# First stage of a transformer block: modulation weights in segments of 256, 384 and 384 features in place of four of 256, with the scale half of each segment used ahead of its shift half

## The chip, the cores and the metric

The kernel runs on one core of a Trainium2 chip. The metric is the time of one execution in device microseconds (us). Executions of an unchanged kernel lie mostly within about 1 us of one another, so medians are quoted with their ranges.

In the profile, PE is TensorE (PEld its weight loads), DVE is VectorE, ACT is ScalarE, POOL is GpSimd, and SPq is the queue that issues the loads. PSUM is the memory that matmuls write to, in banks.

**K** is the start of the first K matmul, **V** the start of the first V matmul.

## The reference

```python
mod = (silu(c) @ w_mod).reshape(..., 6, ...)      # sa, ca, ga, sb, cb, gb: 1024 values each
h = layernorm(x) * (1 + ca) + sa                  # x is 2048 x 1024
x = x + ga * linear_attention(h, wqkv, wo)        # q, k, v = h @ wqkv, 32 heads
h = layernorm(x) * (1 + cb) + sb
x = x + gb * (gelu(h @ w_gate) * (h @ w_up) @ w_down)
```

The first K matmul needs h, h needs the scale ca and the shift sa, and these are two blocks of columns of `silu(c) @ w_mod`. Their weights are 4 MB. So at the start nothing useful can run on TensorE until part of w_mod has been loaded and multiplied.

## The kernel before

The 1024 features are 8 blocks of 128 (called features 0 to 7 here), and a chunk is 128 rows of x. The modulation weights come in four segments of 256 features, each with a shift half (`t=0`) and a scale half (`t=1`). For each segment TensorE runs 32 small matmuls ("passes"; weights 128x128, one moving column), DVE copies the four result columns out of PSUM and adds 0 or 1, DVE modulates the transposed, normalised chunks of x for the two features, and then the K matmuls of these features can run. All K matmuls of chunks 0 to 3 stay open in seven PSUM banks and 496 of the 512 columns of bank 4 until feature 7 is done; the other 16 columns of bank 4 take the results of the passes.

```python
        def wmq_dma(q, ts=(0, 1)):
            for t in ts:
                sch.dma(Q, lambda e, t=t: e.dma_start(WMQ[q][:, :, t, :], wm_v[:, :, t * D + q * 256:t * D + (q + 1) * 256]), ...)
# ... (cut)
        x_dma(0, 1)
        x_dma(1, 2)
        wmq_dma(0, (1,))
        x_dma(2, 3)
        wmq_dma(0, (0,))
        x_dma(3, 4)
        w_dma(WK, OFF_WK, "wk", 1, 0, D, 0, 2)        # Wk, features 0 and 1
        for q in range(1, 4):
            wmq_dma(q)
            # ... Wk of features 2q, 2q+1
# ... (cut)
        def mod_cols(q, bank):       # the 32 passes of a segment
            for t in range(2):
                for b in range(2):
                    for dc in range(NDC):
                        # PS(bank, col) += WMQ[q][:, dc, t, b*128:...] x SILUT[:, dc]
        def mod_copy(q, bank):       # PSUM columns + (0 or 1) -> MODT, on DVE
# ... (cut)
        k_part(0, [2])               # K matmuls of segment 0, chunk 2
        xhat_dve(3, *xh_buf(3))      # normalise chunk 3 (DVE)
        mod_cols(1, 4)
        mod_copy(1, 4)
        t1(3, 7)                     # transpose chunk 3 (PE), copy it out of PSUM (ACT)
        mod1(0, 3, 2, 4)             # modulate chunks 0-2, features 2-3 (DVE)
        k_part(1, [0, 1, 2])
        mod1(3, 1, 0, 4)             # modulate chunk 3, features 0-3
        k_part(0, [3])
        k_part(1, [3])
        mod_cols(2, 4)
        mod_copy(2, 4)
        warm(2)                      # two matmuls on zeros that keep PE busy
        mod1(0, 4, 4, 6)
        k_part(2, [0, 1, 2, 3])
        mod_cols(3, 4)
        mod_copy(3, 4)
        mod1(0, 4, 6, 8)
        # K matmuls of features 6 and 7, then the evacuations and V
```

## Time and profile before

| | before |
|---|---|
| median of 3 runs | 839.61 us (838.99 to 839.78) |
| span of the profiled run | 836.8 us |
| first K matmul (K) | 11.34 |
| first V matmul (V) | 31.57 |
| K to V | 20.23 us |
| V to the end | 805.21 us |

From the page of the kernel before: the span, the busy line, and the first line of the chain of waits (shares of the span by engine).

```profile
span 836.8 us, 11359 instructions
...
PE 830.2 (99%) x4194; PEld 384.4 (46%) x4194; DVE 511.7 (61%) x895; ACT 336.1 (40%) x555; POOL 37.1 (4%) x91
...
PE 98%; DMA 1%; DVE 1%; SPq 0%; ACT 0%; issue 0%
...
```

And the busy times by stretch, from V to the end (columns: stretch, its length, then busy us and instruction count of PE, weight loads, DVE, ACT and POOL, granted clock, DMA share, GB/s):

```profile
...
31.57:837.00 805.43, 802.72 (x3942) 370.19 (x3938) 494.50 (x843) 327.51 (x544) 31.81 (x67) 1.00 0.48 129
...
```

TensorE is busy 802.7 of 805.4 us after V. The longest extra distance between two matmul starts there is 0.1 us. What is left to gain lies ahead of V.

The timeline of PE in the first stage (start, length with the modelled end of the last matmul, what, count, and in brackets idle time and what ended it). L602 are passes, L680 and L756 K (or V) matmuls, L736 warm-up matmuls on zeros, L546 transposes:

```profile
...
9.20 0.95 PE L602 MATMUL ps_all<-siluT,wmq 128*128 128x1 bf16 x32 [0.59 <-DMA wmq<-in_w_mod_dram]
...
11.34 1.02 PE L680 MATMUL ps_all<-wk,h1T 128*128 128x512 bf16 x4
...
14.27 1.04 PE L680 MATMUL ps_all<-wk,h1T 128*128 128x512 bf16 x4 [0.17 <-DVE h1T L565]
15.14 0.94 PE L602 MATMUL ps_all<-siluT,wmq 128*128 128x1 bf16 x32
...
16.76 2.98 PE L680 MATMUL ps_all<-wk,h1T 128*128 128x512 bf16 x13 [0.20 <-DVE h1T L565]
...
21.06 0.94 PE L602 MATMUL ps_all<-siluT,wmq 128*128 128x1 bf16 x32
...
22.71 1.69 PE L680 MATMUL ps_all<-wk,h1T 128*128 128x512 bf16 x7 [0.25 <-DVE h1T L565]
...
26.16 0.94 PE L602 MATMUL ps_all<-siluT,wmq 128*128 128x1 bf16 x32
27.81 3.30 PE L680 MATMUL ps_all<-wk,h1T 128*128 128x512 bf16 x14 [0.71 <-DVE h1T L565]
...
31.57 2.75 PE L680 MATMUL ps_all<-wv,h1T 128*128 128x512 bf16 x12
...
```

Four things are to be seen. The passes of segment 0 wait for their shift load. The first K part starts at 11.34; the trace has Wk's first piece landing at 11.20. Chunk 2's part (14.27) and each of the three later segments (16.76, 22.71, 27.81) begin with idle time that DVE ends. None of these four idle times is a wait for data from memory.

The chain of waits for the last segment (start, length, what):

```profile
...
26.32 0.79 PE ps_all L602 x32
...
27.14 0.17 DVE modt L611
...
27.34 0.42 DVE h1T L565
...
27.81 3.30 PE ps_all L680 x14
...
```

Last pass, 0.17 us copy, 0.42 us for modulating the first feature of four chunks, then K: that round trip is what a segment costs beyond its passes. Bracketed idle times leave out the modelled end of the matmul before, so I count idle time below as the distance between two matmul starts less the usual one (0.216 us after a full matmul, 0.055 after a transpose, 0.025 after a pass). The Trainium skill, "TensorE: Matmul & The Clock Gate", section "Wait — 56ns, not 53.3ns?", has the first (215.7 ns at 512 columns) and the last (a floor of about 25 ns). For before this gives 0.33 us at chunk 2, 0.37 at segment 1, 0.41 at segment 2 (after two warm-up matmuls), 0.85 at segment 3 and 0.11 more at feature 7: 2.07 us.

### The profile page before, as it was taken

How to read it: one execution, taken by the hardware profiler on the slowest of the kernel's cores; microseconds unless marked ns; L12 is line 12 of the kernel's file. 1: busy time of each engine (PE TensorE's matmuls, PEld its weight loads, DVE VectorE, ACT ScalarE, POOL GpSimd, SP SyncE). 2: the span in 40 equal slices, each digit the busy share in tenths (PEclk: the TensorE clock that was granted, in tenths of full speed). 3: DMA queues.
4: the chain of work that ended last, by engine and by line, in shares of the span. 5: the costliest groups of instructions: out<-in, count | busy, mean ns of one | idle time of the engine just before them, and what ended most of it. 6: DMA issues, size and time to landing. Idle time of an engine off the chain costs nothing.

```text
span 836.8 us, 11359 instructions
## 1 busy us (share of the span) xinstructions
PE 830.2 (99%) x4194; PEld 384.4 (46%) x4194; DVE 511.7 (61%) x895; ACT 336.1 (40%) x555; POOL 37.1 (4%) x91
## 2 busy tenths in 40 slices
PE   8999999999999999999999999999999999999998
PEld 4444444444444444444444444444444444444445
DVE  6678877687785577753455665356556535655512
ACT  2357777446423355420354442045554104445300
POOL 2012111000200000010000000000000000000000
DMA  9984422239696769180555533055553305555000
GB/s 291 312 251 101 102 76 76 78 79 235 140 236 204 224 202 277 28 194 26 158 151 151 152 101 76 19 158 152 151 151 101 76 20 159 152 154 145 7 19 26
DMA packets 184102, 113.22 MB, mean 135 GB/s; under 512 B 35560, under 2 KB 175080, under 8 KB 183024
## 3 DMA queue, kind: packets, MB, share of 16 engines
q1 hardware_dynamic: 184032, 112.50, 50.0%
q8 instruction: 33, 0.54, 0.3%
q14 instruction: 21, 0.17, 0.1%
q10 hardware_dynamic: 16, 0.00, 0.0%
HBM read 100.67 MB, written 4.47 MB: 126 GB/s over the span
## 4 chain that ended last, share of the span: by engine, by line
PE 98%; DMA 1%; DVE 1%; SPq 0%; ACT 0%; issue 0%
PE ps_all L1144 23%; PE ps_all L1116 23%; PE ps_all L1119 23%; PE ps_all L680 13%; PE ps_all L1059 7%; PE ps_all L721 7%; PE ps_all L702 1%; DMA wmq<-in_w_mod_dram 1%; PE ps_all L961 0%; PE ps_all L602 0%; DVE h1T L565 0%; PE ps_all L973 0%; PE ps_all L756 0%; PE ps_all L643 0%; SPq L442 0%; DVE st L742 0%
## 5 line engine op out<-in xcount | busy, mean ns | idle before, releaser
L1116 PE MATMUL ps_all<-h2T,wg 128*128 128x512 bf16 x896 | 339.6, 379 | 0.0
L1119 PE MATMUL ps_all<-h2T,wu 128*128 128x512 bf16 x896 | 339.6, 379 | 0.0
L1144 PE MATMUL ps_all<-wd,yT 128*128 128x512 bf16 (+3 forms) x952 | 194.2, 366 | 0.0
L1127 ACT ACTIVATE q<-ps_all 128x512 f32<-128x512 f32 x112 | 66.9, 597 | 225.3 <-PE ps_all L1116 221.5
L1144 PEld LDWEIGHTS ps_all<-wd,yT 128*128 128x128 bf16 x952 | 90.1, 98 | 103.9 <-issue 0.4
L1116 PEld LDWEIGHTS ps_all<-h2T,wg 128*128 128x128 bf16 x896 | 87.7, 98 | 105.8 <-issue 0.2
L1119 PEld LDWEIGHTS ps_all<-h2T,wu 128*128 128x128 bf16 x896 | 87.7, 98 | 105.7
L1132 DVE SCALAR_TENSOR_TENSOR ww<-th,guh 128x512 f32<-128x512 f32 x112 | 77.5, 692 | 77.9 <-ACT th L1131 77.9
L1129 DVE SCALAR_TENSOR_TENSOR ww<-q,ps_all 128x512 f32<-128x512 f32 x112 | 76.9, 686 | 77.7 <-ACT guh L1128 77.6
L1131 ACT ACTIVATE th<-ww 128x512 f32<-128x512 f32 x112 | 70.5, 629 | 87.3 <-DVE ww L1129 87.3
L1149 DVE TENSOR_TENSOR ps_all<-ps_all,gbb 128x512 f32<-128x512 f32 (+3 forms) x34 | 22.7, 667 | 94.8 <-PE ps_all L1144 94.8
L1134 DVE TENSOR_TENSOR yT<-ww,ps_all 128x512 bf16<-128x512 f32 x112 | 76.8, 686 | 3.8
L1128 ACT ACTIVATE guh<-ps_all 128x512 f32<-128x512 f32 x112 | 66.3, 592 | 0.0
L721 PE MATMUL ps_all<-h1T,wq 128*128 128x512 bf16 x256 | 58.7, 379 | 0.0
L680 PE MATMUL ps_all<-wk,h1T 128*128 128x512 bf16 x248 | 57.3, 379 | 1.3 <-DVE h1T L565 1.3
L669 ACT ACTIVATE eb<-ps_all 128x512 f32<-128x512 f32 x64 | 37.4, 600 | 50.6 <-PE ps_all L680 22.3
L680 PE MATMUL ps_all<-wv,h1T 128*128 128x512 bf16 x256 | 57.7, 379 | 0.0
L1059 PE MATMUL ps_all<-w,pq 128*128 128x512 bf16 x256 | 56.2, 379 | 0.0
L670 DVE TENSOR_SCALAR eb<-eb 128x512 f32<-128x512 f32 x64 | 27.1, 423 | 26.7 <-ACT eb L669 26.3
L1059 PEld LDWEIGHTS ps_all<-w,pq 128*128 128x128 bf16 x256 | 25.0, 98 | 30.2 <-issue 0.2
L680 PEld LDWEIGHTS ps_all<-wv,h1T 128*128 128x128 bf16 x256 | 24.9, 98 | 29.5
L680 PEld LDWEIGHTS ps_all<-wk,h1T 128*128 128x128 bf16 x248 | 23.8, 98 | 30.6 <-DVE h1T L565 3.1
(96 smaller groups left out, 481.0 us busy)
## 6 DMA issues: line engine op xcount, KB each, us to landing
wg<-in_B_w_gate_dram SPq DMA_DIRECT2D x56, 512.0 KB, 4.1
wu<-in_B_w_up_dram SPq DMA_DIRECT2D x56, 512.0 KB, 5.3
rb<-scr_rd SPq DMA_DIRECT2D x32, 256.0 KB, 6.6
wd<-in_B_w_down_dram SPq DMA_DIRECT2D x7, 1024.0 KB, 8.5
wmst<-in_w_mod_dram SPq DMA_DIRECT2D x6, 1024.0 KB, 6.8
wmq<-in_w_mod_dram SPq DMA_DIRECT2D x8, 512.0 KB, 7.7
out_dram<-xall SPq DMA_DIRECT2D x31, 128.0 KB, 1.7
xall<-in_A_x_dram SPq DMA_DIRECT2D x3, 1024.0 KB, 12.4
```

The source lines that it names most:

```text
L680: o = sch.op(T, lambda e, dc=dc: e.matmul(PS(bank), H1[sg][:, dc, ci * P:(ci + 1) * P], W_[:, dc, jg * 512:(jg + 1) * 512], start=(dc == 0 ...
L721: o = sch.op(T, lambda e, dc=dc: e.matmul(PS(b), WQ[:, dc, qc * P:(qc + 1) * P], H1[sg][:, dc, :], start=(dc == 0), stop=(dc == NDC - 1)), ...
L1059: last[half] = sch.op(T, lambda e, g=g, half=half: e.matmul(PS(b0 + half), PQ[sg][:, g, ci * P:(ci + 1) * P], W2[:, g, half * 512:(half + ...
L1116: og = sch.op(T, lambda e, dc=dc: e.matmul(PS(bg), WG[slot][:, dc, e_ * P:(e_ + 1) * P], H2[sg][:, dc, :], start=(dc == 0), stop=(dc == ND ...
L1119: ou = sch.op(T, lambda e, dc=dc: e.matmul(PS(bu), WU[slot][:, dc, e_ * P:(e_ + 1) * P], H2[sg][:, dc, :], start=(dc == 0), stop=(dc == ND ...
L1127: sch.op(A, lambda e: e.activation(Q1[j][:, :], PS(bg), ACTF.Square, scale=math.sqrt(GELU_A)), prd=pr(bg), wr=rq, note=f"q1 {fc}")
L1128: ogh = sch.op(A, lambda e: e.activation(GUH[j][:, :], PS(bg), ACTF.Copy, scale=0.5), prd=pr(bg), wr=rg, note=f"gh {fc}")
L1129: sch.op(V, lambda e: e.scalar_tensor_tensor(WW[j][:, :], Q1[j][:, :], 1.0, PS(bg), op0=ALU.add, op1=ALU.mult), rd=rq, prd=pr(bg), wr=rw, ...
L1131: sch.op(A, lambda e: e.activation(TH[j][:, :], WW[j][:, :], ACTF.Tanh, scale=GELU_C), rd=rw, wr=rt, note=f"th {fc}")
L1132: sch.op(V, lambda e: e.scalar_tensor_tensor(WW[j][:, :], TH[j][:, :], 1.0, GUH[j][:, :], op0=ALU.add, op1=ALU.mult), rd=rt + rg, wr=rw, n ...
L1134: sch.op(V, lambda e: e.tensor_tensor(YT[:, fc, :], WW[j][:, :], PS(bu), ALU.mult), rd=rw, prd=pr(bu), wr=r_yt(fc), note=f"yT {fc}")
L1144: o = sch.op(T, lambda e, b=b, fc=fc, c0=c0, c1=c1, n=n: e.matmul(PS(b, 0, n), YT[:, fc, ci * P:(ci + 1) * P], WDT[fc // 4][:, fc % 4, c0:c1],
```

## The change

Three segments of 2, 3 and 3 features need one round of copy and modulation less. Each scale half is multiplied ahead of its shift half, without waiting for it. Loads of 384 features have 768 B packets in place of 512 B. To have K work between the two halves, chunk 3's transpose moves ahead of segment 1, and its K parts of features 0 and 1 stand between the halves. Two smaller parts: after each later copy DVE modulates chunk 0 alone first, and one K matmul of chunk 3 is kept back as filler behind the last copy.

```diff
-        WMQ = [at(f"wmq{i}", [P, NDC, 2, 256], bf16, MSO[i]) for i in range(4)]
+        SEG = [(0, 2), (2, 5), (5, 8)]
+        SGO = [OFF_MS3, OFF_WS, OFF_WS + 12288]
+        WMQ = [at(f"wmq{i}", [P, NDC, 2, (d1 - d0) * P], bf16, SGO[i]) for i, (d0, d1) in enumerate(SEG)]
 # ... (loads: scale, then shift, of each segment, then its Wk features; cut)
         warm(6, 7)
-        mod_cols(0, 4)
+        mod_cols(0, 1, 4)
+        mod_cols(0, 0, 4)
 # ... (cut)
         xhat_dve(3, *xh_buf(3))
-        mod_cols(1, 4)
-        mod_copy(1, 4)
         t1(3, 7)
-        mod1(0, 3, 2, 4)
-        k_part(1, [0, 1, 2])
-        mod1(3, 1, 0, 4)
+        mod1(3, 1, 0, 2)
+        mod_cols(1, 1, 4)
         k_part(0, [3])
         k_part(1, [3])
-        mod_cols(2, 4)
-        mod_copy(2, 4)
+        mod_cols(1, 0, 4)
+        mod_copy(1, 4)
+        mod1(0, 1, 2, 3)
+        mod1(1, 3, 2, 3)
+        mod1(0, 4, 3, 5)
         warm(2)
-        mod1(0, 4, 4, 6)
-        k_part(2, [0, 1, 2, 3])
-        mod_cols(3, 4)
-        mod_copy(3, 4)
+        k_part(2, [0, 1, 2, 3])
+        k_part(3, [0, 1, 2, 3])
+        mod_cols(2, 1, 4)
+        k_part(4, [0, 1, 2])
+        mod_cols(2, 0, 4)
+        mod_copy(2, 4)
+        mod1(0, 1, 5, 6)
+        mod1(1, 3, 5, 6)
         mod1(0, 4, 6, 8)
+        kv_mm(3, "k", 0, kb0[3, 0], [4])
+        k_part(5, [0, 1, 2])
+        kv_mm(3, "k", 0, kb0[3, 0], [5])
 # ... (features 6 and 7, and chunk 3's second half of features 4 to 7; cut)
```

In the new kernel `k_part` takes one feature, not a segment of two.

More of the change, by code (lines that the diff above doesn't have):

```diff
@@ L297, in bass_adaLN_cond__linear_attn_block__geglu_ffn__prompt_kernel @@
             ("c8", [NDC, P], bf16, 256), ("cT", [P, NDC], f32, 64), ("chalf", [P, NDC], f32, 64),
-            ("thc", [P, NDC], f32, 64), ("siluT", [P, NDC], bf16, 64), ("modt", [P, 16], f32, 64), ("add4", [P, 4], f32, 64),
+            ("thc", [P, NDC], f32, 64), ("siluT", [P, NDC], bf16, 64), ("modt", [P, 16], f32, 64), ("add6", [P, 6], f32, 64),
             ("sbT", [P, NDC], f32, 64), ("cb1T", [P, NDC], f32, 64),
@@ L312, in bass_adaLN_cond__linear_attn_block__geglu_ffn__prompt_kernel @@
         SBT, CB1T, CBT, ZCOLS = (_small[k] for k in ("sbT", "cb1T", "cbT", "zcols"))
-        MODT, ADD4 = _small["modt"], _small["add4"]
+        MODT, ADD6 = _small["modt"], _small["add6"]
         NEGHALF, STA, MVA, RSA, NMA, VEA = (_small[k] for k in ("neghalf", "st", "mv", "rs", "nm", "ve"))
@@ L357, in r_wmq @@
         def r_wmq(i, t):
-            return [(MSO[i] + (dc * 2 + t) * 512, MSO[i] + (dc * 2 + t + 1) * 512, f"wmq{i}") for dc in range(NDC)]
+            w = (SEG[i][1] - SEG[i][0]) * P * 2
+            return [(SGO[i] + (dc * 2 + t) * w, SGO[i] + (dc * 2 + t + 1) * w, f"wmq{i}") for dc in range(NDC)]
         R_WARM = [(OFF_GUH, OFF_GUH + 1024, "warm")]
@@ L449, in w_dma, with wmq_dma @@
                            wr=[t_ for dc in range(dc0, dc1) for t_ in r_w(off, name, dc, c0, c1)], note=f"{name}.{dc0}.{c0}")
-        def wmq_dma(q, ts=(0, 1)):
-            for t in ts:
-                sch.dma(Q, lambda e, t=t: e.dma_start(WMQ[q][:, :, t, :], wm_v[:, :, t * D + q * 256:t * D + (q + 1) * 256]),
-                        wr=r_wmq(q, t), note=f"wmq{q}.{t}")
+        def wmq_dma(q, t):
+            d0, d1 = SEG[q]
+            sch.dma(Q, lambda e: e.dma_start(WMQ[q][:, :, t, :], wm_v[:, :, t * D + d0 * P:t * D + d1 * P]), wr=r_wmq(q, t), note=f"wmq{q}.{t}")
         sch.op(V, lambda e: e.memset(WARM[:], 0.0), wr=R_WARM, note="warm")
-        sch.op(V, lambda e: e.memset(ADD4[:, 0:2], 0.0), wr=r_sm("add4"), note="add4")
-        sch.op(V, lambda e: e.memset(ADD4[:, 2:4], 1.0), wr=r_sm("add4"), note="add4")
+        sch.op(V, lambda e: e.memset(ADD6[:, 0:3], 0.0), wr=r_sm("add6"), note="add6")
+        sch.op(V, lambda e: e.memset(ADD6[:, 3:6], 1.0), wr=r_sm("add6"), note="add6")
         x_dma(0, 1)
         x_dma(1, 2)
-        wmq_dma(0, (1,))
+        wmq_dma(0, 1)
         x_dma(2, 3)
-        wmq_dma(0, (0,))
+        wmq_dma(0, 0)
         x_dma(3, 4)
         w_dma(WK, OFF_WK, "wk", 1, 0, D, 0, 2)
-        for q in range(1, 4):
-            wmq_dma(q)
-            for d0, d1 in ((2, 4),) if q == 1 else ((2 * q, 2 * q + 1), (2 * q + 1, 2 * q + 2)):
+        for q, ds in ((1, ((2, 4), (4, 5))), (2, ((5, 6), (6, 7), (7, 8)))):
+            wmq_dma(q, 1)
+            wmq_dma(q, 0)
+            for d0, d1 in ds:
                 w_dma(WK, OFF_WK, "wk", 1, 0, D, d0, d1)
@@ L575, in mods_act, with r_modt @@
                        rd=r_h1(sg, dc, dc + 1, s0, s1) + rs_, wr=r_h1(sg, dc, dc + 1, s0, s1), note=f"h1moda {sg}.{s0}.{dc}")
+        SEGD = [(q, d0, d1) for q, (d0, d1) in enumerate(SEG) for _ in range(d0, d1)]
+        def r_modt(q):
+            d0, d1 = SEG[q]
+            return [(SMO["modt"] + 8 * d0, SMO["modt"] + 8 * d1, "modt")]
         def sc1(dc):
-            k = (dc // 2) * 4 + dc % 2
-            return MODT[:, k + 2:k + 3], MODT[:, k:k + 1], r_smc("modt", dc // 2, 16)
+            q, d0, d1 = SEGD[dc]
+            k = d0 + dc
+            return MODT[:, k + d1 - d0:k + d1 - d0 + 1], MODT[:, k:k + 1], r_modt(q)
         def sc2(dc):
@@ L593, in bass_adaLN_cond__linear_attn_block__geglu_ffn__prompt_kernel, with mod_cols @@
         MC0 = 496
-        def mod_cols(q, bank):
+        def mod_cols(q, t, bank):
             o = None
-            rng = [(bank * 2048 + (MC0 + q * 4) * 4, bank * 2048 + (MC0 + q * 4 + 4) * 4)]
-            for t in range(2):
-                for b in range(2):
-                    col = MC0 + q * 4 + t * 2 + b
-                    for dc in range(NDC):
-                        o = sch.op(T, lambda e, t=t, b=b, dc=dc, col=col: e.matmul(
-                            PS(bank, col, col + 1), WMQ[q][:, dc, t, b * P:(b + 1) * P], SILUT[:, dc:dc + 1],
-                            start=(q == t == b == dc == 0), stop=(dc == NDC - 1), skip_group_check=True),
-                            rd=r_wmq(q, t) + r_sm("siluT"), pwr=(rng if dc == 0 else ()), note=f"mod{q}.{t}.{b}.{dc}")
+            d0, d1 = SEG[q]
+            c0 = MC0 + 2 * d0 + t * (d1 - d0)
+            rng = [(bank * 2048 + c0 * 4, bank * 2048 + (c0 + d1 - d0) * 4)]
+            for b in range(d1 - d0):
+                for dc in range(NDC):
+                    o = sch.op(T, lambda e, b=b, dc=dc: e.matmul(
+                        PS(bank, c0 + b, c0 + b + 1), WMQ[q][:, dc, t, b * P:(b + 1) * P], SILUT[:, dc:dc + 1],
+                        start=(q == b == dc == 0 and t == 1), stop=(dc == NDC - 1), skip_group_check=True),
+                        rd=r_wmq(q, t) + r_sm("siluT"), pwr=(rng if dc == 0 else ()), note=f"mod{q}.{t}.{b}.{dc}")
             for t_ in rng:
@@ L609, in mod_copy @@
         def mod_copy(q, bank):
-            rng = [(bank * 2048 + (MC0 + q * 4) * 4, bank * 2048 + (MC0 + q * 4 + 4) * 4)]
-            sch.op(V, lambda e: e.tensor_tensor(MODT[:, q * 4:q * 4 + 4], PS(bank, MC0 + q * 4, MC0 + q * 4 + 4), ADD4[:, :], ALU.add),
-                   prd=rng, rd=r_sm("add4"), wr=r_smc("modt", q, 16), note=f"modcp{q}")
+            d0, d1 = SEG[q]
+            n = d1 - d0
+            rng = [(bank * 2048 + (MC0 + 2 * d0) * 4, bank * 2048 + (MC0 + 2 * d1) * 4)]
+            sch.op(V, lambda e: e.tensor_tensor(MODT[:, 2 * d0:2 * d1], PS(bank, MC0 + 2 * d0, MC0 + 2 * d1), ADD6[:, 3 - n:3 + n], ALU.add),
+                   prd=rng, rd=r_sm("add6"), wr=r_modt(q), note=f"modcp{q}")
         MT = (4, 5, 6, 7, 8, 9)
@@ L761, in k31, with k_part @@
                 sch.ps.set_writer(*rng[0], o)
-        def k_part(q, cs):
-            for dc in (2 * q, 2 * q + 1):
-                for (c_, jg), b in kb0.items():
-                    if c_ in cs:
-                        kv_mm(c_, "k", jg, b, [dc])
-                if 3 in cs:
-                    k31([dc])
+        def k_part(dc, cs):
+            for (c_, jg), b in kb0.items():
+                if c_ in cs:
+                    kv_mm(c_, "k", jg, b, [dc])
+            if 3 in cs:
+                k31([dc])
         warm(11, 7)
@@ L791, in bass_adaLN_cond__linear_attn_block__geglu_ffn__prompt_kernel @@
         k_part(0, [0])
+        k_part(1, [0])
         xhat_dve(2, *xh_buf(2))
@@ L798, in bass_adaLN_cond__linear_attn_block__geglu_ffn__prompt_kernel @@
         k_part(0, [1])
+        k_part(1, [1])
         mod1(2, 1, 0, 2)
@@ L801, in bass_adaLN_cond__linear_attn_block__geglu_ffn__prompt_kernel @@
         k_part(0, [2])
+        k_part(1, [2])
         xhat_dve(3, *xh_buf(3))
-        mod_cols(1, 4)
-        mod_copy(1, 4)
         t1(3, 7)
-        mod1(0, 3, 2, 4)
-        k_part(1, [0, 1, 2])
-        mod1(3, 1, 0, 4)
+        mod1(3, 1, 0, 2)
+        mod_cols(1, 1, 4)
         k_part(0, [3])
         k_part(1, [3])
-        mod_cols(2, 4)
-        mod_copy(2, 4)
-        warm(2)
-        mod1(0, 4, 4, 6)
-        k_part(2, [0, 1, 2, 3])
-        mod_cols(3, 4)
-        mod_copy(3, 4)
+        mod_cols(1, 0, 4)
[3 more added lines that the diff above has]
+        mod1(0, 4, 3, 5)
+        warm(2)
+        k_part(2, [0, 1, 2, 3])
[3 more added lines that the diff above has]
+        mod_cols(2, 0, 4)
+        mod_copy(2, 4)
+        mod1(0, 1, 5, 6)
+        mod1(1, 3, 5, 6)
         mod1(0, 4, 6, 8)
+        kv_mm(3, "k", 0, kb0[3, 0], [4])
+        k_part(5, [0, 1, 2])
+        kv_mm(3, "k", 0, kb0[3, 0], [5])
         for (c_, jg), b in kb0.items():
             kv_mm(c_, "k", jg, b, [6, 7])
-        k31([6, 7])
+        k31([4, 5, 6, 7])
         k31(list(range(NDC)), MC0, 512)
```

## The prediction

> **What bounds the kernel now.** TensorE: the page has PE busy 99% of the span, the chain of waits 98% PE. Listing PE instructions by start, from the first V matmul (31.57 us) to the end there is no idle over 0.1 us. So only the first stage can move the time: total = start of V + 805 us. The change touches nothing after it.
>
> The first stage, before (timeline): warm-up; wait for the first w_mod segment (landed 9.15, passes at 9.20); first K matmul at 11.33, when the first Wk piece had just landed (11.20); then only latency chains. PE idles 0.34 us before chunk 2's K part, 0.2 in each of segments 1 and 2 (warm-up matmuls hide more of the latter), 0.7 before segment 3. These chains are: last pass, copy to modt, modulation on DVE, K matmul, about 0.8 us each. Nothing on PE after 11.33 waits for a DMA.
>
> **What the change does.** Pass count stays 128 (25 ns apart, the floor that the Trainium skill states in "TensorE: Matmul & The Clock Gate", section "Wait — 56ns, not 53.3ns?"; the trace agrees), K matmuls 64 at 216 ns, warm-ups 25. Removed: one copy/modulate round of four. The scale half of each segment runs before the shift half lands. DMA: 4 MB still, but 768 B packets in four loads. From 27 ns at 512 B and 46 at 1 KB in the trace I estimate 37 ns at 768 B: 2.4 us per load, about 1 us less DMA time in all.
>
> **On the critical path.** Estimates from trace durations, in the new PE order:
> - Segment 0 finishes 0.4 us earlier, but four warm-ups follow and the first K matmul still needs Wk, landing 11.20: K starts at 11.3, gain at most 0.1. Chunk 2's part still starts near 14.2-14.3 (ACT copy 1.02 us, then DVE).
> - T1 of chunk 3 follows directly (15.1), then 24 scale passes (0.6), then chunk 3's K parts of features 0-1. These need the transpose drained, the ACT copy (1.02) and DVE (0.3): ready at 17.1-17.2, PE free at 16.1. A new bubble of about 1.0 us.
> - 24 shift passes, to 18.65; copy, modulate chunk 0 alone (128 wide, 0.31); K at 19.4, idle 0.3 after two warm-ups.
> - 16 K matmuls, 24 passes, 6 K, 24 passes, to 25.35; one K matmul as filler, idle 0.5; K of feature 5 at 26.1; 7+14+4 matmuls and the 16-column rest: V at 31.6-31.7.
>
> The saved round (about 0.7 us) pays for the new bubble and little remains: net -0.2 to +0.3 us. Estimated landings leave over 1 us of slack at every later load (shift of segment 1 lands at 16.0, needed 18; of segment 2 at 22.9, needed 24.8), also with the 1.5 us by which one DMA engine lagged before, after a 16 KB instruction fetch.
>
> **Prediction: 839.6 us**, 838.6 to 840.6 in 8 of 10. Faster by over 2%: 0.003; within 2%: 0.994; slower by over 2%: 0.003.
>
> **What would show it.** V's first matmul at 31.4-31.9; first K at 11.3; a PE gap of 1 us before chunk 3's first K matmul, released by DVE modulation; gaps of 0.3 and 0.5 after the two later copies; 768 B packets near 37 ns; no PE wait on a DMA after 11.33; the rest unchanged.
>
> **What would make it wrong.** 768 B packets costing as much as 1 KB (46 ns): the last shift load would land at 25-27 and stall PE up to 2 us. The warm-up ending at another moment. A lowered PE clock after the longer stretch of small passes and idle at 15-17 us. A gain of 0.5-1 us if chunk 3's transpose, copy and modulation overlap better than I count.

## More of the kernel before

`k31`, which `k_part` calls for chunk 3 (not shown), is the second half of chunk 3's K. It shares PSUM bank 4 with the pass results, so it may not run while DVE copies those out.

## The result, and the profile after

| | before | after |
|---|---|---|
| median of 6 runs | 839.3 us (838.66 to 839.78) | 839.02 us (838.69 to 839.51) |
| ratio | | 0.9997, 95% interval 0.9984 to 1.001 |
| span of the profiled run | 836.8 | 837.7 |
| first Wk piece lands | 11.20 | 11.99 |
| K | 11.34 | 12.12 |
| V | 31.57 | 32.49 |
| K to V | 20.23 | 20.37 |
| V to the end | 805.21 | 805.21 |

A ratio is the mean time of one kernel's runs over that of the other's of the same rounds, so not quite the ratio of the medians.

The profiled execution of after is even 0.9 us longer than that of before, of which 0.78 lies ahead of K. The repeats below show that this part is chance. The page of after, then its stretch from V to the end:

```profile
span 837.7 us, 11356 instructions
...
PE 829.8 (99%) x4194; PEld 384.5 (46%) x4194; DVE 511.4 (61%) x894; ACT 336.4 (40%) x555; POOL 36.8 (4%) x91
...
PE 98%; DMA 1%; SPq 1%; DVE 0%; ACT 0%; issue 0%
...
```

```profile
...
32.49:838.00 805.51, 802.73 (x3942) 370.31 (x3939) 494.23 (x842) 327.36 (x543) 31.55 (x67) 1.00 0.48 128
...
```

After V nothing has moved: 802.73 us of matmuls against 802.72. The timeline of PE (L612 passes, L692 and L768 K matmuls, L748 warm-ups, L549 transposes):

```profile
...
8.37 0.54 PE L612 MATMUL ps_all<-siluT,wmq 128*128 128x1 bf16 x16
9.94 0.55 PE L612 MATMUL ps_all<-siluT,wmq 128*128 128x1 bf16 x16 [1.03 <-DMA wmq<-in_w_mod_dram]
...
12.12 1.02 PE L692 MATMUL ps_all<-wk,h1T 128*128 128x512 bf16 x4 [0.30 <-DMA wk<-in_A_wqkv_dram]
...
15.06 1.04 PE L692 MATMUL ps_all<-wk,h1T 128*128 128x512 bf16 x4 [0.17 <-DVE h1T L568]
15.93 0.61 PE L549 MATMUL ps_all<-ident,xh 128*128 128x128 bf16 x8
16.38 0.74 PE L612 MATMUL ps_all<-siluT,wmq 128*128 128x1 bf16 x24
18.01 0.39 PE L692 MATMUL ps_all<-wk,h1T 128*128 128x512 bf16 x1 [0.89 <-DVE h1T L568]
...
18.87 0.74 PE L612 MATMUL ps_all<-siluT,wmq 128*128 128x1 bf16 x24
...
20.22 1.69 PE L692 MATMUL ps_all<-wk,h1T 128*128 128x512 bf16 x7 [0.15 <-DVE h1T L568]
...
25.56 0.74 PE L612 MATMUL ps_all<-siluT,wmq 128*128 128x1 bf16 x24
...
26.91 4.71 PE L692 MATMUL ps_all<-wk,h1T 128*128 128x512 bf16 x21 [0.37 <-DVE h1T L568]
...
32.49 1.67 PE L692 MATMUL ps_all<-wv,h1T 128*128 128x512 bf16 x7
...
```

The last 16 passes of segment 0 still wait for the shift load, and K waits 0.30 us for Wk (0.46 by the count above). After the transpose of chunk 3 (15.93) and the 24 scale passes (16.38) stands the new hole: 0.89 us, ended by DVE. The two later rounds show 0.15 and 0.37 us in place of three of 0.20, 0.25 and 0.71. The chain of waits through the hole:

```profile
...
16.10 0.46 PE ps_all L549 x8
...
16.58 1.03 ACT h1T L551
...
17.64 0.33 DVE h1T L568
...
18.01 0.39 PE ps_all L692
...
```

Transpose, then 1.03 us of ACT copying it out of PSUM, then 0.33 us of DVE, then K. Only 0.6 us of passes stand against that.

Counted as above: 0.33 us at chunk 2 (unchanged), 1.03 in the hole, 0.31 at segment 1, 0.53 at segment 2: 2.20 us against 2.07. The difference, 0.13, is the 0.14 us by which K to V grew. Split up: three rounds of before cost 0.37 + 0.41 + 0.95 = 1.73, two of after 0.84. The change saves 0.89 us and gives back 1.03.

### The profile page after: what moved, and what is told of

Its sections match the earlier page's. It is cut to its first block, busy times and chain, and to the rows that moved or that the text cites. A ratio compares the mean times of both kernels' runs of the same rounds, so it can differ in the third digit from the quotient of the medians.

```text
span 837.7 us, 11356 instructions
## 1 busy us (share of the span) xinstructions
PE 829.8 (99%) x4194; PEld 384.5 (46%) x4194; DVE 511.4 (61%) x894; ACT 336.4 (40%) x555; POOL 36.8 (4%) x91
## 4 chain that ended last, share of the span: by engine, by line
PE 98%; DMA 1%; SPq 1%; DVE 0%; ACT 0%; issue 0%
PE ps_all L1166 23%; PE ps_all L1138 23%; PE ps_all L1141 23%; PE ps_all L692 13%; PE ps_all L1081 7%; PE ps_all L733 7%; PE ps_all L714 1%; DMA wk<-in_A_wqkv_dram 1%; SPq L445 0%; PE ps_all L983 0%; ACT h1T L551 0%; PE ps_all L995 0%; PE ps_all L768 0%; PE ps_all L612 0%; PE ps_all L655 0%; SPq L456 0%
## 5 line engine op out<-in xcount | busy, mean ns | idle before, releaser
L692 PE MATMUL ps_all<-wk,h1T 128*128 128x512 bf16 x248 | 57.1, 379 | 1.9 <-DVE h1T L568 1.6
L692 PE MATMUL ps_all<-wv,h1T 128*128 128x512 bf16 x256 | 57.7, 379 | 0.0
L692 PEld LDWEIGHTS ps_all<-wv,h1T 128*128 128x128 bf16 x256 | 24.9, 98 | 29.5
L692 PEld LDWEIGHTS ps_all<-wk,h1T 128*128 128x128 bf16 x248 | 23.8, 98 | 31.1 <-DVE h1T L568 3.3
```

The source lines that it names most:

```text
L692: o = sch.op(T, lambda e, dc=dc: e.matmul(PS(bank), H1[sg][:, dc, ci * P:(ci + 1) * P], W_[:, dc, jg * 512:(jg + 1) * 512], start=(dc == 0 ...
```

## The experiments

Theory A is the one of the prediction: the order of work on PE decides, and the new hole eats the saved round. Rival B: loads decide (the change delays Wk, or PE is bound by landings). Rival C: the split into halves does nothing because PE waits for the shift load anyway (together), or Wk's landing does nothing because modulation on DVE binds K (swap). Rival D stands for two opposite things: in oldorder, fewer segments save nothing, since each larger load lands later; in four, fewer rounds are what counts.

| run | median us | before, same rounds | ratio (95%) | Wk lands | K | V | K to V |
|---|---|---|---|---|---|---|---|
| rep_before | 839.57 | 839.05 | 1.0004 (0.9991-1.0016) | 12.18 | 12.32 | 32.55 | 20.23 |
| before_swap | 839.03 | 839.05 | 0.9994 (0.9982-1.0006) | 11.10 | 11.79 | 32.03 | 20.24 |
| rep_after | 839.27 | 839.2 | 0.9998 (0.9986-1.001) | 11.46 | 11.60 | 31.98 | 20.38 |
| rep_after2 | 838.8 | 839.03 | 0.9996 (0.9983-1.0008) | 11.05 | 11.18 | 31.56 | 20.38 |
| together | 839.69 | 839.2 | 1.0005 (0.9993-1.0017) | 11.59 | 11.72 | 32.70 | 20.98 |
| swap | 838.62 | 839.2 | 0.9991 (0.9979-1.0003) | 10.61 | 11.16 | 31.57 | 20.41 |
| fill | 838.35 | 839.2 | 0.9985 (0.9973-0.9997) | 12.05 | 12.18 | 31.41 | 19.23 |
| oldorder | 838.7 | 839.05 | 0.9998 (0.9982-1.0013) | 11.87 | 12.01 | 31.31 | 19.30 |
| fillswap | 838.16 | 839.05 | 0.9978 (0.9965-0.9991) | 10.49 | 11.16 | 31.23 | 20.06 |
| fillswap2 | 838.19 | 839.03 | 0.9985 (0.9973-0.9998) | 10.99 | 11.44 | 31.17 | 19.74 |
| four | 837.41 | 839.03 | 0.9978 (0.9964-0.9991) | 11.09 | 11.23 | 30.70 | 19.48 |

All gave correct results. Where the interval leaves out 1 the difference is clear of the noise. Five rounds were run for each.

### The two kernels again

No edit: the kernel after twice, the kernel before once.

> The changed kernel again. Theory A (the saved round is paid for by the new bubble ahead of chunk 3's K parts; nothing after the first stage moves): ratio to before 0.999 to 1.001, and from the first K matmul to the first V matmul again about 20.3-20.4 us (20.37 in the first profile; 20.23 in the profile of before), whatever moment the first Wk piece lands. Rival B (the change made the first Wk piece land later, 11.99 against 11.20, and would gain without that): Wk lands near 12.0 again and V starts at 32.5 again. If Wk lands near 11.2 here, the 0.8 us between the two profiles was chance.

> The changed kernel a third time, beside the two above on one chip: ratio 1.000 within 0.1%; first K to first V 20.37-20.41.

> The kernel before, profiled again. Theory A: first K to first V 20.2 us as in the first profile, ratio 1.000; the landing of the first Wk piece differs from profile to profile of one kernel (it was 12.0 and 11.5 us in two profiles of the changed kernel, 11.2 in the one of before). Rival B (the new loads delay the first Wk piece): 11.2 again.

K to V repeats to 0.01 us: 20.23 and 20.23 for before, 20.37, 20.38 and 20.38 for after. What does not repeat is the moment when Wk's first piece lands: 11.20 and 12.18 in the two profiles of before, 11.99, 11.46 and 11.05 in the three of after. In all eight profiles with these opening loads (fill, oldorder and together have them too) K follows Wk by 0.13 to 0.14 us. The first part of rival B, that the change delays Wk, falls: in the repeats it is before that is late. The 0.9 us between the two first profiles is a drawn lot, not the change.

### together: the scale passes back beside the shift passes

```diff
-        mod_cols(1, 1, 4)
         k_part(0, [3])
         k_part(1, [3])
+        mod_cols(1, 1, 4)
         mod_cols(1, 0, 4)
```

> Changed kernel with segment 1's scale passes put back next to its shift passes, after chunk 3's K parts. Theory A: the 24 passes (0.60 us) then no longer run inside the bubble but after it: bubble 1.05 -> 1.65 us, V 0.6 us later relative to the first K matmul (21.0 against 20.37), total +0.6 us. Rival C (the split does nothing, PE waits for the shift load anyway): no change in the distance from first K to first V.

The PE timeline:

```profile
...
15.53 0.61 PE L549 MATMUL ps_all<-ident,xh 128*128 128x128 bf16 x8
17.61 0.39 PE L692 MATMUL ps_all<-wk,h1T 128*128 128x512 bf16 x1 [1.47 <-DVE h1T L568]
...
18.47 1.34 PE L612 MATMUL ps_all<-siluT,wmq 128*128 128x1 bf16 x48
...
```

The hole grew to 1.47 us in brackets (1.63 by my count against 1.03), the 48 passes then run in one go, and K to V is 20.98: 0.60 us more than the 20.38 of rep_after, the time of 24 passes. Rival C falls for this part: the shift load had landed at 16.39, so PE did not wait for it. Early scale passes are worth exactly the idle time they run in. The rest of the hole shows that there is not enough of such work.

### fill: all of segment 1's passes into the hole

```diff
         mod_cols(1, 1, 4)
-        k_part(0, [3])
-        k_part(1, [3])
         mod_cols(1, 0, 4)
         mod_copy(1, 4)
+        kv_mm(3, "k", 0, kb0[3, 0], [0, 1])
         mod1(0, 1, 2, 3)
         mod1(1, 3, 2, 3)
         mod1(0, 4, 3, 5)
-        warm(2)
-        k_part(2, [0, 1, 2, 3])
+        k_part(2, [0, 1, 2])
+        kv_mm(3, "k", 0, kb0[3, 0], [2])
+        k31([0, 1, 2])
```

Chunk 3's second half (`k31`) could not serve as filler, since PE would write PSUM bank 4 while DVE reads the pass results from it. (The Trainium skill, "PSUM — Partial Sum Buffer", section "PSUM bank collisions raise a hardware error", has a hardware error for two engines on one bank and the same 32 partitions at once. No run here shows it.)

> Changed kernel with segment 1's shift passes and copy pulled ahead of chunk 3's K parts, so that passes fill the bubble, and two warm-ups dropped for two K matmuls as filler. Theory A: the gap of 1.05 us before chunk 3's K parts falls to about 0.4 and first K to first V shrinks by 0.9-1.1 us (to about 19.3) if the shift load of segment 1 has landed by then (needs about 5.0 us after the first K matmul); total -0.9 us or so. Rival B (the stage is bound by DMA landings): PE now waits for that shift load and the gain is 0.3 us or less.

The PE timeline:

```profile
...
15.99 0.61 PE L549 MATMUL ps_all<-ident,xh 128*128 128x128 bf16 x8
16.44 1.34 PE L612 MATMUL ps_all<-siluT,wmq 128*128 128x1 bf16 x48
18.07 2.33 PE L692 MATMUL ps_all<-wk,h1T 128*128 128x512 bf16 x9 [0.29 <-DVE h1T L568]
...
```

48 passes run where 24 did, the hole is 0.29 us in brackets (0.43 by my count), and K to V is 19.23: 1.14 us less than in after, a little over the range of theory A. The hole gives 0.60 of this. The rest is the round that followed: its 0.31 us of idle time becomes 0.20 (at 18.71), and the two warm-up matmuls (0.43 us) go. Dropping them alone from after would save nothing by its trace: behind them PE is idle until DVE has modulated, and the chain of waits runs through passes, copy and modulation, not through them:

```profile
...
19.47 0.59 PE L748 MATMUL ps_all<-warm 128*128 128x512 bf16 x2
...
```

(This line is from the timeline of after; its next K matmuls are the line at 20.22 above.) The shift load of segment 1 landed at 16.86, before PE came to its passes at about 17.05, so no load bound here. Rival B's second part falls for this kernel. The executions agree: 838.35 against 839.27 us for the changed kernel of the same rounds.

### oldorder: three segments in the order of the kernel before

```diff
         xhat_dve(3, *xh_buf(3))
-        t1(3, 7)
-        mod1(3, 1, 0, 2)
         mod_cols(1, 1, 4)
-        k_part(0, [3])
-        k_part(1, [3])
         mod_cols(1, 0, 4)
         mod_copy(1, 4)
-        mod1(0, 1, 2, 3)
-        mod1(1, 3, 2, 3)
-        mod1(0, 4, 3, 5)
-        warm(2)
-        k_part(2, [0, 1, 2, 3])
-        k_part(3, [0, 1, 2, 3])
+        t1(3, 7)
+        mod1(0, 3, 2, 5)
+        k_part(2, [0, 1, 2])
+        mod1(3, 1, 0, 5)
+        k_part(3, [0, 1, 2])
+        for dc in range(4):
+            k_part(dc, [3])
```

> Changed kernel's three segments and loads, but around segment 1 the order of the kernel before: both passes and the copy ahead of chunk 3's transpose, chunk 3's K parts after those of chunks 0 to 2. Theory A (fewer rounds do save time, the place of chunk 3's K parts gives it back): no bubble of 1 us; PE waits up to 0.4 us for the shift load of segment 1 (it lands about 4.7 us after the first K starts); first K to first V about 19.3 us, 1.0 us under the changed kernel; total -0.9 us. Rival D (fewer segments save nothing, since each larger load lands later): first K to first V about 20.2.

The PE timeline:

```profile
...
15.82 0.74 PE L612 MATMUL ps_all<-siluT,wmq 128*128 128x1 bf16 x24
16.72 0.75 PE L612 MATMUL ps_all<-siluT,wmq 128*128 128x1 bf16 x24 [0.16 <-DMA wmq<-in_w_mod_dram]
17.33 0.61 PE L549 MATMUL ps_all<-ident,xh 128*128 128x128 bf16 x8
18.20 2.96 PE L692 MATMUL ps_all<-wk,h1T 128*128 128x512 bf16 x13 [0.26 <-DVE h1T L568]
...
```

The second 24 passes do wait for the shift load (0.30 us by my count; it landed at 16.67), the transpose of chunk 3 fills part of the copy's round trip, and chunk 3's K parts run when their data has long been ready. K to V is 19.30, as theory A said, and 0.93 us less than in the kernel *before*. So three segments (with the split halves and the one matmul of filler that the change gave to segment 2) do save time. By the count above, the round that is left out gave 0.84 us (0.41 idle and two warm-up matmuls), the last round costs 0.42 less (its filler and its narrower first modulation), and segment 1 costs 0.35 more, of which 0.30 is the wait for the load. So the rival D of this run falls, by a sum of gaps and not by a run that changes the number of segments alone. It was the place given to chunk 3 that took the gain away. The executions do not settle it: two of six took 840.66 and 841.74 us, the other four 837.73 to 838.77. Before had such high ones in the same rounds too (841.03, 841.34), and all four of these show a clock of 0.998, so they are not put down to this kernel. Without them the means are 838.38 (four) and 839.12 us (nine), a ratio of 0.9991; but that choice was made after the fact, so the statement rests on the trace.

### swap and before_swap: Wk ahead of chunk 3's x

```diff
-        x_dma(3, 4)
         w_dma(WK, OFF_WK, "wk", 1, 0, D, 0, 2)
+        x_dma(3, 4)
```

> Changed kernel with the first Wk piece loaded ahead of chunk 3's x. Theory A: in the changed kernel the first K matmul waits for Wk alone (0.3 us idle before it in the profile), so Wk landing 0.7 us earlier lets K start right after the four warm-ups, 0.3-0.4 us earlier, and V with it (chunk 3's x is not needed before about 0.5 us after it lands); total -0.3 us. Rival C (K's start is bound by modt and DVE): no change.

> The kernel before with the first Wk piece ahead of chunk 3's x, as in the swap run. Theory A: in the kernel before all 32 passes of segment 0 run after its shift half lands, 0.4 us later, so the PE reaches the first K matmul just about when Wk lands; with Wk 0.7 us earlier K still starts 2.1 us after that shift half lands, so little gain: 0 to -0.2 us in total. Rival (Wk alone bound the start in both kernels equally): -0.4 us or more, as the swap did for the changed kernel.

In the timeline of swap (the changed kernel with this edit) K follows the four warm-up matmuls without a wait:

```profile
...
10.30 1.03 PE L748 MATMUL ps_all<-warm 128*128 128x512 bf16 x4
11.16 1.03 PE L692 MATMUL ps_all<-wk,h1T 128*128 128x512 bf16 x4
...
```

The landing of the load that all of this hangs on differs from execution to execution, so K is compared with the landing of segment 0's shift half. In after K came 2.22 us behind it (9.90), in swap 1.89 us behind it (9.27): 0.33 us earlier (the repeats of after have 2.20 and 2.17, so 0.28 at the least). In the kernel before it came 2.19 us behind it (2.22 in the repeat), in before_swap 2.17 (9.62): next to nothing gained. That is what theory A asks for. In before, 32 passes and Wk end at about the same time. In after, the early scale passes finish segment 0 by 0.4 us sooner, and Wk, whose place in the queue was not changed, hides all of it. Rival C falls here too. K to V is within 0.04 us of that without the swap in both. The totals are too near each other to tell.

### fillswap, twice: both edits

> Both the fill and the swap edits: the candidate that should beat both kernels. Theory A: the gains add, first K at about 11.0-11.2 and first K to first V 19.2, V at 30.3, total -1.3 us against before, unless the shift load of segment 2 (23.5 to 24.2 us in the last profiles) now arrives after PE gets to it (about 23.45): then V is 7.0 us after that landing, 30.5 to 31.2, and DMA has become the limit.

> Repeat of fillswap on another chip or hour: ratio 0.998 to 0.999; V again 7.0 us after the shift load of segment 2 lands, or 19.2 us after the first K, whichever is later.

The gains did not add. In the first run K was at 11.16 as hoped, but K to V was 20.06, not 19.2. The chain of waits of fillswap (from the first run) says why:

```profile
...
12.40 11.84 DMA wmq<-in_w_mod_dram
...
24.28 0.77 PE ps_all L612 x24
...
25.07 0.17 DVE modt L623
...
25.27 0.33 DVE h1T L568
...
25.65 4.71 PE ps_all L692 x21
...
```

PE was now at the last passes before their load, which landed at 24.24, and the chain ahead of 24.28 is the load and nothing else. V is 6.99 us behind that landing in both runs (24.24 and 31.23; 24.18 and 31.17), which is the second alternative. Of the stage, a load has become the limit: that is where rival B is right. But it is one late part of a load. A load has landed when the last of its sixteen parts has, one for each DMA engine, and the trace has a time for each. Fifteen parts of this load had landed by 22.77 us (23.22 in the second run), and PE was ready at about 23.8; the sixteenth came 1.47 us (0.96) later. PE waited 0.79 us for segment 2's loads in the first run and 0.47 in the second. Less these waits K to V would be 19.27 in both, an estimate, so near to fill's 19.23 that the gains of the two edits do add where no part of a load is late. The ratios, 0.9978 and 0.9985, are nevertheless under 1 in both intervals.

### four: four segments with the lessons

This is the kernel with segments of 256 again, swap's loads, and chunk 3's K matmuls as filler behind the later copies. The core of the edit against before:

```diff
         k_part(2, [0, 1, 2])
+        k_part(3, [0, 1, 2])
         mod1(3, 1, 0, 4)
-        k_part(0, [3])
-        k_part(1, [3])
-        mod_cols(2, 4)
+        k31([0, 1, 2, 3])
+        mod_cols(2, 1, 4)
+        mod_cols(2, 0, 4)
         mod_copy(2, 4)
-        warm(2)
+        kv_mm(3, "k", 0, kb0[3, 0], [0, 1, 2, 3])
         mod1(0, 4, 4, 6)
 # ... (segment 3 likewise: chunk 2's feature 5 and chunk 3's features 4, 5 as filler; cut)
```

(`k_part` counts features here, as in the kernel after.)

> Four segments of 256 again (as before), but with the early scale passes, the swapped first loads, and K matmuls of chunk 3 kept back as filler behind each copy. If theory A is right that the order of work on PE decides and not the number of segments, this does better than three segments although it has one round more: first K to first V about 18.7 us if the last shift load lands in time, otherwise V about 5.1 us after that landing (so 30.3 for a landing at 25.2); total -1.4 to -2 us against before. Rival D (fewer rounds are what counts): no better than the fill run, 19.2 us.

V came at 30.70, 5.08 us behind the last shift load's landing (25.62), which is the second alternative's number; but PE came to the passes of that load only at about 25.69, so it was just in time and did not bind. The first alternative, 18.7 us, was missed for two other waits. Segment 2's shift load landed at 21.40, and PE stood 0.53 us for it (idle in the timeline's brackets, 0.66 by my count); fifteen of its sixteen parts had landed by 19.51, and PE was ready at about 20.8, so this too was one late part. And segment 1's K matmuls, whose first data DVE had modulated by 16.60, began at about 16.95 (counted back from the next group, since one record is missing), 0.13 us after their Wk had landed at 16.82; the profile names DVE there, but the landing fits and DVE does not. The two lines of the timeline:

```profile
...
17.17 2.54 PE L692 MATMUL ps_all<-wk,h1T 128*128 128x512 bf16 x11 [0.72 <-DVE h1T L568]
...
21.44 0.55 PE L612 MATMUL ps_all<-siluT,wmq 128*128 128x1 bf16 x16 [0.53 <-DMA wmq<-in_w_mod_dram]
...
```

With a median of 837.41 us against 839.03 of before and 838.8 of after in the same rounds it has the lowest median and the earliest V, although it has one round more than after. (Its executions, 836.92 to 838.16 us, overlap those of fillswap2, 837.2 to 838.35, so these two are not told apart by them.) So a gain here does not need fewer segments; it needs work to put behind each copy. The rival D of this run (no better than fill, 19.2 us) is not refuted: K to V is 19.48 against fill's 19.23. Without the 0.66 us of the late load it would be 18.8 (an estimate), but no run shows that. What stands is that four rounds with filler take 0.75 us less from K to V than the four rounds of before.

## Why the prediction was right

The prediction was 839.6 us, between 838.6 and 840.6; measured were 839.02, 839.27 and 838.8 us. That the total fell into the range tests little: the medians of before_swap, together, swap and oldorder, 838.62 to 839.69 us, lie in it too. What tests the prediction are the times of the first stage.

- *Only the start of V counts.* Shown: 805.21 or 805.22 us from V to the end in all 13 profiles.
- *The saved round pays for the new hole.* Shown by the traces: 0.89 us saved, 1.03 given back, K to V +0.14 us. The term for the saved round, "about 0.7", was 0.2 too small; the hole, "about 1.0", was right, as were the "0.3 and 0.5" of the two later copies (0.31 and 0.53). together, fill and oldorder each move the hole and K to V follows, by +0.60, -1.14 and -1.07 us; in fill and oldorder 0.43 us of this are the two warm-up matmuls that go with the round.
- *Segment 0's earlier passes gain at most 0.1 us, because Wk binds.* Shown: K waits 0.30 us for Wk in the timeline, and the swap frees 0.33 us in after and none in before.
- *768 B packets cost about 37 ns.* Their median in the trace of after is 36 ns, their mean 39.9, and a load of 768 KB takes 2.4 us as estimated. No load after K is waited for in after.
- *V at 31.4 to 31.9, K at 11.3, no wait for a load after that.* In the first profile V was 32.49 and K 12.12, after a wait for Wk, all off; in the others V was 31.98 and 31.56, K 11.60 and 11.18. Only the third kept to the range (its 31.56), and that is luck with Wk. The step that was mis-sized is the landing of Wk, taken as fixed at 11.20 from one profile. It ran from 11.05 to 12.18 in the eight profiles that have the same opening loads. It touches both kernels alike, so the ratio did not suffer.

Whether after is really 0.1 us slower than before, as K to V says, or 0.2 us faster, as three ratios just under 1 would have it, is below what these runs resolve. Why Wk lands where it does in a given execution stays open as well.

## What to carry to other kernels

Before taking a synchronisation round out, look at what stands in the place it leaves: a step moved forward to fill the gap may itself have a chain behind it (here 0.46 us of transposes, 1.03 us of ACT copy and 0.33 us of DVE) that needs more filler than there is. Keep matmuls whose operands have long been ready for the places behind a copy, and put work with a fresh dependency last. And when a stage's order has been mended, expect a load to become its limit: compare the landing of each load with the time at which its user is ready before adding up gains, and look at the last of its parts.

## What the Trainium skill lacked or had wrong

- "DMA: Bandwidth & Descriptors", section "Specifications", gives 512 B as the least transfer for line rate. In the trace of before, up to 60 us, the median packet takes 27 ns at 512 B, 46 at 1 KB and 84 at 2 KB, so 19, 22 and 24 B/ns per engine: at 512 B it is a fifth under the rate at 2 KB. The 768 B packets of after have a median of 36 ns, 21 B/ns (its 1 KB packets 49 ns, so a median can differ by 3 ns between two traces).
- The same page's section "Why small descriptors are slow (HBM only)" has a fixed cost for each packet, which agrees with this direction. It does not say what such a load takes as a whole: 512 KB in 512 B packets landed 1.4 to 1.8 us behind the load before it in most cases, 768 KB in 768 B packets 2.3 to 2.5 us in most.
- No page says that a fetch of instructions delays a kernel's loads; it would belong to "Runtime: NRT & Kernel Launch", section "Instruction fetch mechanics". A packet of 16 KB on the instruction queue took 1.21 us at 16.7 us in before. The loads that follow landed 1.5 us later on one of the sixteen engines than on most of the others (19.48 against 17.93 and under), and a load counts only when the last has landed. Each of the thirteen profiles has such a packet, of 1.09 to 1.21 us, between 16.2 and 21.7 us. In eight of them the last of a load's sixteen parts falls behind the one before it by 0.38 to 1.55 us more at one of the next two loads than ahead of the packet; in the other five by 0.23 us at most. The trace does not name the DMA engine, so that this packet is the cause is argued from its time and length alone.
- No page that I found gives the scatter of landings for one and the same series of loads: the seventh, Wk, landed between 11.05 and 12.18 us in eight profiles.
